# Block-causal attention with a gated MLP on one core: transposes behind the row maxima, transfers at once, an earlier first MLP, spread weight work

## The chip, the core and the metric

The kernel runs on one core of a Trainium2 chip. The time is device microseconds of one execution. The engines are named as in the profile: PE (TensorE, matrix products; PEld its weight loads), DVE (VectorE), ACT (ScalarE), POOL (GpSimd) and SP (SyncE, which here only issues transfers). Each engine executes its own instruction list in order; a semaphore makes an instruction wait for work of another engine.

## What is computed

For 8 batches and 8 heads (S = 576 positions, 64 numbers per head), scores = q kT / 8 with a mask by blocks of 64 (a row of block i sees the blocks up to i), softmax over a row, product with v. The heads side by side are x, 576 x 512 per batch. Then the gated MLP:

```python
h = np.maximum(x @ w_in, 0.0)               # 512 -> 1024
u, v = (h[..., :d_ff // 2], h[..., d_ff // 2:])
mu = np.mean(v, axis=-1, keepdims=True)
var = np.mean((v - mu) ** 2, axis=-1, keepdims=True)
v_n = (v - mu) / np.sqrt(var + 1e-06)
v_s = np.einsum('ts,bsd->btd', w_spatial, v_n) + b_spatial[None, :, None]
gated = u * v_s
return (gated @ w_out).astype(np.float32)   # 512 -> 512
```

Most products are made in three parts: an operand is split into a high part (a rounded copy, made by ACT) and a low part (the rest, made by POOL or DVE), and high x high, high x low and low x high are summed in PSUM.

## The kernel before

**Pairs and slots.** A batch has four pairs of heads; pair (b, p) is done in seven slots (`NS = 7`), one per step of the loop over `n`. Slots 0 to 5 are row tiles 0-1, 2 and 3 of the one and of the other head, slot 6 is what is left of both heads (two halves of 288 columns). For a slot PE makes the scores (L285, L297), DVE the row maximum (L320, or L329 for slot 6; `exps`), which also copies the scores out of PSUM into a tile p, ACT the exponential (L336), DVE the sum and its reciprocal (L347, L350; `norm`), POOL the scaling of p (L354), DVE the transpose in 32 x 32 blocks into a tile q (`transposes`, L406, L411). When a pair has all its slots transposed, 16 transfers (`move`, L421) put the quarters of q into place in the one buffer `turned`, from which PE makes the product with v (`av`, L464 and L481). ACT and DVE take that out of PSUM as high and low part of x (`x_evac`, L439, L443). Batch 0 and the very last pair transpose on PE instead (`transposes_pe`, L383) and have the scores from unsplit operands (batch 0). Scores have four PSUM banks, which are taken in turn; all other products share four more. Tiles p have five buffers, `turned` one.

**The MLP.** A batch has 29 groups of matmuls: five of v (`v_group`, L512, L522), eight of u (L606), eight of the spatial product (`sp_group`, L630 to L635) and eight of the output (L665). `begin(b)` puts them in a queue; in each step a credit grows by `rate` and lets groups go, so that the MLP of one batch lies between the scores of the next. What follows a group on the other engines is put into later steps with `later(steps, phase, f)`, and `due(phase)` carries it out at four places of a step. After a v group ACT evacuates (L530), DVE makes the statistics (L542, L543 and a chain of small instructions), ACT normalises (L566) and copies the high part, DVE makes the low part (L582; L586 for the fifth group, whose 64 rows go to `vs_a` and `vs_b`). The tiles of v before normalisation, tag `vr`, share their buffers with the weights that are being converted.

**Weights and operands.** `spread(gen, count, first, last)` deals the sub-steps of a generator evenly over steps. The weights are 64-bit words; DVE converts them to 32 bits (L145 to L158), ACT makes the high part and POOL the low part (L122, L124). `prep_pair` splits the next pair's operands (ACT L240, POOL L243).

**Order.** The program is written in steps, but a scheduler that knows the dependencies puts the instructions of each engine into the order in which they stand; on the chip that order is fixed. The step's core is:

```python
            exps(*here, i)
        if at(n - 1) and (i - 1) % NS in (1, 3, 5, 6):
            norm(*at(n - 1))
        due(1)
        step_background(n)
```

## Time and profile before

| | |
|---|---|
| median of 3 runs | 764.27 us (762.53 to 765.03) |
| profiled execution | 762.24 us, span 760.4 us |
| PE busy | 717.2 us, 94% |
| DVE, ACT, POOL busy | 459.7, 425.8 and 339.4 us |
| transfers | 92.05 MB, mean 121 GB/s |

"Busy" leaves out issuing, branches and semaphores. The window rows that are shown below have, after the stretch and its length, the busy time of PE, PEld, DVE, ACT and POOL with the number of instructions, the granted clock of TensorE (1.00 is full), the mean share of the transfer engines, and GB/s. A row of waits reads: waiting engine and instruction, what it waited for, total us, count, longest. A timeline row has the start, the length, the engine, line, operation and tiles; in brackets stands how long the engine stood idle before it, and for what. Line numbers are those of the kernel before.

### The profile page before, as it was taken

The numbers are of one execution on the slowest core, as the hardware profiler recorded it, in microseconds if no ns is written. First come the engines' busy times: TensorE is split into PE (matmuls) and PEld (weight loads), VectorE is DVE, ScalarE is ACT, GpSimd is POOL, SyncE is SP. The second block draws the span as 40 slices with busy tenths as digits, with TensorE's granted clock in tenths as the row PEclk, the third lists the DMA queues.
The fourth block names the chain that finished last, engine by engine and source line by source line (L and its number), as shares of the span: only waits on it lengthen the run. The fifth ranks groups of instructions, "written<-read, shape, count | busy, mean of one in ns | idle before, by whom it ended". The sixth has DMA issues, their size and how long they took to land.

```text
span 760.4 us, 16376 instructions
## 1 busy us (share of the span) xinstructions
PE 717.2 (94%) x5729; PEld 621.4 (82%) x5729; DVE 459.7 (60%) x1587; ACT 425.8 (56%) x1156; POOL 339.4 (45%) x525
## 2 busy tenths in 40 slices
PE   8879858999989999899999999899998999999998
PEld 5647747888878888798888988798887988899897
DVE  6985876556676557756665557756576557621430
ACT  6877754445654555655565556754566556642542
POOL 4788456553325633555136534355335551231011
PEclk9999969899999999999999999999999999999999
DMA  6443624355435554455353753345553552341001
GB/s 215 163 151 96 185 89 135 91 157 161 111 93 145 160 159 102 105 151 143 107 136 94 198 146 92 110 135 146 157 136 86 152 156 65 97 105 41 7 16 47
DMA packets 42150, 92.05 MB, mean 121 GB/s; under 512 B 9298, under 2 KB 18002, under 8 KB 42068
## 3 DMA queue, kind: packets, MB, share of 16 engines
q1 hardware_dynamic: 32852, 81.56, 39.1%
q10 hardware_dynamic: 9216, 9.44, 3.7%
q8 instruction: 45, 0.74, 0.4%
q14 instruction: 37, 0.30, 0.1%
HBM read 38.18 MB, written 9.44 MB: 63 GB/s over the span
## 4 chain that ended last, share of the span: by engine, by line
PE 50%; DVE 16%; ACT 15%; POOL 10%; issue 6%; DMA 1%; SPq 0%; POOLq 0%; DVEq 0%; ACTq 0%
PE mo L665 13%; PE ms L630 11%; PE s L285 7%; ACT p L336 5%; POOL lo L243 4%; PE avh L464 4%; POOL p L354 4%; PE mv L512 4%; PE mu L606 3%; ACT vr L566 3%; DVE p L320 3%; DVE st L542 3%; DVE q L406 2%; PE avl L464 2%; PE s L297 2%
## 5 line engine op out<-in xcount | busy, mean ns | idle before, releaser
L354 POOL TENSOR_SCALAR p<-p,ssum 128x128 f32<-128x128 f32 (+4 forms) x288 | 159.0, 567 | 206.4 <-DVE ssum L350 100.1
L336 ACT ACTIVATE p<-p,nmax 128x128 f32<-128x128 f32 (+4 forms) x288 | 167.0, 581 | 87.4 <-DVE nmax L320 43.5
L406 DVE STREAM_TRANSPOSE q<-p 128x384 f32<-128x384 f32 (+1 forms) x189 | 114.0, 623 | 69.4 <-POOL p L354 65.3
L320 DVE CUSTOM_DVE_ANT_0 p<-s,mask 128x128 f32<-128x128 f32 (+3 forms) x256 | 117.8, 477 | 31.9 <-PE s L285 29.0
L243 POOL TENSOR_TENSOR lo<-raw,hi 128x288 fp32r<-128x288 f32 x112 | 94.3, 865 | 90.4 <-ACT hi L240 90.4
L606 PE MATMUL mu<-x,wi_hi 128*128 128x288 f32 x512 | 115.6, 304 | 0.0
L649 POOL TENSOR_TENSOR gl<-u,gh 128x288 fp32r<-128x288 f32 x64 | 51.4, 806 | 91.4 <-ACT gh L648 91.3
L606 PEld LDWEIGHTS mu<-x,wi_hi 128*128 128x128 f32 x512 | 86.3, 190 | 5.2 <-issue 1.2
L512 PE MATMUL mv<-wi_hi,x 128*128 128x512 f32 x256 | 85.3, 395 | 0.0
L630 PE MATMUL ms<-ws_hi,vh 128*128 128x288 f32 x256 | 77.1, 301 | 6.9 <-DVE x L443 6.9
L665 PE MATMUL mo<-gh,wo_hi 128*128 128x288 f32 x256 | 79.2, 309 | 0.0
L665 PE MATMUL mo<-gl,wo_hi 128*128 128x288 f32 x256 | 77.0, 301 | 1.7 <-POOL gl L649 1.4
L648 ACT CAST gh<-u 128x288 fp32r<-128x288 f32 x64 | 27.5, 433 | 87.9 <-DVE u L639 82.5
L285 PE MATMUL s<-hi 64*128 64x128 f32 (+1 forms) x224 | 64.5, 404 | 12.6 <-DVE nmax L329 6.1
L665 PE MATMUL mo<-gh,wo_lo 128*128 128x288 f32 x256 | 75.6, 295 | 0.0
L630 PE MATMUL ms<-ws_hi,vl 128*128 128x288 f32 x256 | 75.5, 295 | 0.0
L630 PE MATMUL ms<-ws_lo,vh 128*128 128x288 f32 x256 | 75.4, 294 | 0.0
L606 PE MATMUL mu<-x,wi_lo 128*128 128x288 f32 x256 | 70.6, 298 | 0.0
L639 DVE TENSOR_TENSOR u<-ms,u 128x288 f32<-128x288 f32 x64 | 28.3, 445 | 53.7 <-PE ms L635 53.7
L285 PEld LDWEIGHTS s<-hi 64*128 64x128 f32 x224 | 31.7, 188 | 35.5 <-issue 14.3
L512 PEld LDWEIGHTS mv<-wi_hi,x 128*128 128x128 f32 x256 | 48.1, 188 | 11.3 <-ACT st L545 1.5
L464 PE MATMUL avh<-turned,v 128*64 128x128 f32 x868 | 56.7, 285 | 0.0
(120 smaller groups left out, 1608.9 us busy)
## 6 DMA issues: line engine op xcount, KB each, us to landing
turned<-q SPq DMA_DIRECT2D x216, 100.0 KB, 2.2
turned<-q SPq DMA_DIRECT2D x216, 96.0 KB, 2.2
raw<-qk SPq DMA_DIRECT2D x31, 608.0 KB, 4.3
v<-v SPq DMA_DIRECT2D x32, 320.0 KB, 3.1
outT<-o ACTq DMA_DIRECT2D x64, 144.0 KB, 2.3
rwi<-w_in SPq DMA_DIRECT2D x8, 512.0 KB, 3.7
rwo<-w_out SPq DMA_DIRECT2D x4, 512.0 KB, 4.4
rws<-w_spT SPq DMA_DIRECT2D x4, 288.0 KB, 2.8
```

What stands on the lines that cost most here:

```text
L243: nc.gpsimd.tensor_tensor(out=lo[:, cs], in0=raw[:, cs], in1=hi[:, cs].bitcast(F32), op=ALU.subtract)
L285: nc.tensor.matmul(banks[(b, pr, i + hd)][:, o:o + n], a[js, qs], k[js, :n], start=(m == 0), stop=(m == len(parts) - 1),)
L320: nc.vector.tensor_tensor_reduce(out=pt[:, o:o + n], in0=bk[:, o:o + n], in1=mask[:, 512 - n:], scale=-0.125, scalar=BIG, op0=ALU.add, op1 ...
L336: nc.scalar.activation(pt[:, o:o + n], pt[:, o:o + n], AF.Exp, bias=mx, scale=-1.0, accum_out=ssum[:, s0 + r:s0 + r + 1],)
L354: nc.gpsimd.tensor_scalar(out=pt[:, o:o + w], in0=pt[:, o:o + w], scalar1=ssum[:, r:r + 1], scalar2=1.0, op0=ALU.mult, op1=ALU.mult,)
L406: nc.vector.transpose(to[:, :, o:o + 32 * n].rearrange("p r (c j) -> p c r j", j=32), pt[:, :n * P].rearrange("p (c r j) -> p c r j", r=4, ...
L464: nc.tensor.matmul(out[js, (t0 - q0) * P:(t1 + 1 - q0) * P].rearrange("p (t a j) -> p a t j", a=4, j=32), vt[:, c, js], src[:, :, o:o + 32 ...
L512: nc.tensor.matmul(ps, xs[k][:, j, cs], w[:, k, DH:], start=(n == 0), stop=(n == 3 * NC - 1),)
L606: nc.tensor.matmul(ps[:, :HT], w[:, k, ds], xs[k][:, j, zs], start=(n == 0), stop=(n == 3 * NC - 1),)
L630: nc.tensor.matmul(ps[:, :HT], a[:, ds], w[:, k, zs], start=(n == 0), stop=False)
L649: nc.gpsimd.tensor_tensor(out=gl[:, dc, :], in0=uz, in1=gh[:, dc, :].bitcast(F32), op=ALU.subtract)
L665: nc.tensor.matmul(ps[:, :HT], w[:, k, es], a[:, k, :], start=(n == 0), stop=(n == 3 * ND - 1),)
```

## The change

Six edits. (1) The block transposes of a pair's slot are issued one step later (`n - 3`) and directly behind the row maxima and exponentials of the step, where they stood at the end of the step. (2) The 16 transfers of a pair are issued together; they were dealt out four per step. (3) `av` is issued ahead of the maxima, and in batch 0 the evacuation of x, the copy of its tail and `begin` come a step sooner each, so that the first batch's MLP starts two steps sooner. (4) The weights' sub-steps get other ranges: the v half of w_in steps 2 to 18 (before: 3 to 20), the u half 18 to 33 (21 to 34), w_sp 33 to 40 (33 to 39); w_out has its old range. (5) In `prep_pair` both high copies are one sub-step, and the low parts start after two. (6) The tag `vr` has two buffers, before three.

```diff
@@ -31,8 +31,7 @@
-LAST, AV_AT, BOOT_AV, MOVES = 5, 2 * NS + 2, NS + 2, 4
+LAST, AV_AT, BOOT_AV = 5, 2 * NS + 2, NS + 2
@@ -137,7 +136,7 @@
-        f = ff_p.tile([P, 512], F32, tag="vr", name=f"f{name}", bufs=3)[:, :n]
+        f = ff_p.tile([P, 512], F32, tag="vr", name=f"f{name}", bufs=2)[:, :n]
@@ -238,7 +237,8 @@
         for cs in (slice(0, S), slice(S, KQ)):
             nc.scalar.copy(hi[:, cs], raw[:, cs])
-            yield
+        yield
+        yield
@@ -419,7 +419,6 @@
             for a in range(4):
                 nc.sync.dma_start(turned[32 * r:32 * r + 32, a, :w], t[32 * a:32 * a + 32, r, :w])
-                yield
@@ -444,6 +443,10 @@
+        if b == 0:
+            hi()
+            lo()
+            return
         later(1, 0, hi)
         later(1, 1, lo)
@@ -486,7 +489,7 @@
-        later(1, 2, lambda: nc.gpsimd.tensor_scalar(
+        later(1 if b else 0, 2, lambda: nc.gpsimd.tensor_scalar(
             out=tails[b][:, pr], in0=xts[(b, pr)][:, :, FULL * P:].bitcast(F32), scalar1=1.0,
             scalar2=1.0, op0=ALU.mult, op1=ALU.mult,
         ))
@@ -500,7 +503,7 @@
-            vr = ff_p.tile([P, DH], F32, tag="vr", name=f"vr_{b}_{c}", bufs=3)
+            vr = ff_p.tile([P, DH], F32, tag="vr", name=f"vr_{b}_{c}", bufs=2)
@@ -725,14 +728,13 @@
     load_pair(0, 0)
     load_v(0, 0)
     U0 = NPAIR * NS
-    spread(chain([prep_w_in(c, 1) for c in range(NC)]), 7 * NC + 1, 3, U0 - 8)
-    spread(chain([prep_w_in(c, 0) for c in range(NC)]), 7 * NC + 1, U0 - 7, U0 + 6)
-    spread(chain([prep_w_sp(c) for c in range(FULL)] + [prep_w_tail()]), 3 * FULL + 5, U0 + 5, U0 + 11)
+    spread(chain([prep_w_in(c, 1) for c in range(NC)]), 7 * NC + 1, 2, 18)
+    spread(chain([prep_w_in(c, 0) for c in range(NC)]), 7 * NC + 1, 18, U0 + 5)
+    spread(chain([prep_w_sp(c) for c in range(FULL)] + [prep_w_tail()]), 3 * FULL + 5, U0 + 5, U0 + 12)
     spread(chain([prep_w_out(c) for c in range(ND)]), 7 * ND + 1, U0 + 10, U0 + 17)
     queue = []
     rate = 0.0
     credit = 0.0
-    moving = []
 
 
     TURNS = ((), (0, 1), (), (2, 3), (), (4, 5), (6,))
@@ -771,7 +773,7 @@
             if i == LAST + 1 and g + 2 < NPAIR:
                 load_pair(0, g + 2)
             if i == 2 and b > 0:
-                spread(prep_pair(b, pr), 7, n, n + 4)
+                spread(prep_pair(b, pr), 8, n, n + 4)
         if i == 3 and NPAIR < g < len(pairs):
             load_v(*pairs[g - 1])
         if i == 4 and here == last:
@@ -786,35 +788,32 @@
                 scores(*here, (4, 5))
             elif i == LAST:
                 scores_last(*here)
+        for of in range(max(0, g - 2), min(g + 1, len(pairs))):
+            if n - of * NS == (BOOT_AV if by_pe(pairs[of]) else AV_AT):
+                av(*pairs[of])
+                if of % NPAIR == NPAIR - 1:
+                    later(1 if of >= NPAIR else 0, 3, lambda b=pairs[of][0]: begin(b))
+        if here:
             exps(*here, i)
+        if at(n - 3):
+            for j in TURNS[(i - 3) % NS]:
+                b, pr, _ = at(n - 3)
+                if not by_pe((b, pr)):
+                    transposes(b, pr, j)
+                    if j == NS - 1:
+                        move(b, pr)
         if at(n - 1) and (i - 1) % NS in (1, 3, 5, 6):
             norm(*at(n - 1))
         due(1)
         step_background(n)
-        for of in range(max(0, g - 2), min(g + 1, len(pairs))):
-            if n - of * NS == (BOOT_AV if by_pe(pairs[of]) else AV_AT):
-                av(*pairs[of])
-                if of % NPAIR == NPAIR - 1:
-                    later(1, 3, lambda b=pairs[of][0]: begin(b))
-        for gen in moving[:1]:
-            for _ in range(MOVES):
-                if next(gen, gen) is gen:
-                    moving.remove(gen)
-                    break
-        turn = [(*at(n - 2)[:2], j) for j in TURNS[(i - 2) % NS]] if at(n - 2) else []
-        for b, pr, j in turn:
-            if by_pe((b, pr)):
-                transposes_pe(b, pr, j)
+        if at(n - 2) and by_pe(at(n - 2)[:2]):
+            for j in TURNS[(i - 2) % NS]:
+                transposes_pe(*at(n - 2)[:2], j)
         credit = min(credit + rate, 2.0)
         while credit >= 1.0 and queue and queue[0][0]():
             queue.pop(0)[1]()
             credit -= 1.0
         due(2)
-        for b, pr, j in turn:
-            if not by_pe((b, pr)):
-                transposes(b, pr, j)
-                if j == NS - 1:
-                    moving.append(move(b, pr))
         due(3)
 
 
```

The order on DVE where batch 2's MLP ends its v and u groups and its spatial groups begin, under pairs (3,3) and (4,0); `ms_2_0_0` is the first spatial product, `q_3_3` the transposed p of pair (3,3), `x_3_1` the x of pair (3,1), whose PSUM banks `avl`, `avh` it frees. Before:

```order
L320 ISA p_4_0_0_4179,nmax_4_0_0_4177<-s_4_0_0_4163,mask_93 128x256
L320 ISA nmax_4_0_0_4177 128x1
L406 STREAM_TRANSPOSE q_3_3_4055<-p_3_3_4_4061 128x4x4x32
L347 TENSOR_SCALAR ssum_3_3_6_4132<-ssum_3_3_6_4132 128x1
L443 TENSOR_TENSOR x_3_1_4023<-avl_3_1_3974,x_3_1_4023 128x256
L443 TENSOR_TENSOR x_3_1_4023<-avh_3_1_3975,x_3_1_4023 128x320
L350 RECIPROCAL ssum_3_3_6_4132<-ssum_3_3_6_4132 128x1
L406 STREAM_TRANSPOSE q_3_3_4055<-p_3_3_5_4103 128x4x4x32
L639 TENSOR_TENSOR u_2_3525<-ms_2_0_0_4039,u_2_3525 128x288
```

And of the change:

```order
L442 TENSOR_TENSOR x_3_1_4052<-avl_3_1_3972,x_3_1_4052 128x256
L329 ISA p_3_3_6_4151,nmax_3_3_6_4149<-s_3_3_6_0_4117,mask_93 128x288
L329 ISA nmax_3_3_6_4149 128x1
L406 STREAM_TRANSPOSE q_3_3_4090<-p_3_3_2_4004 128x3x4x32
L329 ISA p_3_3_6_4151,nmax_3_3_6_4149<-s_3_3_6_1_4118,mask_93,nmax_3_3_6_4149 128x288
L329 ISA nmax_3_3_6_4149 128x1
L406 STREAM_TRANSPOSE q_3_3_4090<-p_3_3_3_4057 128x3x4x32
L347 TENSOR_SCALAR ssum_3_3_4_4086<-ssum_3_3_4_4086 128x2
L442 TENSOR_TENSOR x_3_1_4052<-avh_3_1_3973,x_3_1_4052 128x320
```

The two instructions that make the low half of x stood between the transposes of slots 4 and 5; now they stand ahead of the transpose of slot 4, among the row maxima of slot 6 and the transposes of slots 2 and 3.

A little earlier on DVE, the row maxima of slots 2 to 4 of pair (3,3) and the low half `vs_a` of the fifth v group of batch 2. Before:

```order
L320 ISA p_3_3_2_3962,nmax_3_3_2_3960<-s_3_3_2_3921,mask_93 128x384
L320 ISA nmax_3_3_2_3960 128x1
L560 TENSOR_SCALAR st_2_4_3825<-st_2_4_3825 64x1
L320 ISA p_3_3_3_4028,nmax_3_3_3_4027<-s_3_3_3_3922,mask_93 128x384
L320 ISA nmax_3_3_3_4027 128x1
L347 TENSOR_SCALAR ssum_3_3_0_3890<-ssum_3_3_0_3890 128x4
L350 RECIPROCAL ssum_3_3_0_3890<-ssum_3_3_0_3890 128x4
L320 ISA p_3_3_4_4061,nmax_3_3_4_4059<-s_3_3_4_3952,mask_93 128x512
L320 ISA nmax_3_3_4_4059 128x1
L586 TENSOR_TENSOR vs_a_118<-vr_2_4_3824,vs_b_119 64x512
```

And of the change:

```order
L320 ISA p_3_3_1_3943,nmax_3_3_1_3942<-s_3_3_1_3896,mask_93 128x256
L320 ISA nmax_3_3_1_3942 128x1
L589 TENSOR_TENSOR vs_a_118<-vr_2_4_3812,vs_b_119 64x512
L320 ISA p_3_3_2_4004,nmax_3_3_2_4002<-s_3_3_2_3934,mask_93 128x384
L320 ISA nmax_3_3_2_4002 128x1
L320 ISA p_3_3_3_4057,nmax_3_3_3_4056<-s_3_3_3_3935,mask_93 128x384
L320 ISA nmax_3_3_3_4056 128x1
L347 TENSOR_SCALAR ssum_3_3_0_3910<-ssum_3_3_0_3910 128x4
L350 RECIPROCAL ssum_3_3_0_3910<-ssum_3_3_0_3910 128x4
L320 ISA p_3_3_4_4087,nmax_3_3_4_4085<-s_3_3_4_3964,mask_93 128x512
L320 ISA nmax_3_3_4_4085 128x1
```

`vs_a` stood behind the maximum of slot 4 and now stands ahead of that of slot 2; the statistics of the same group, which stood among the maxima of slots 0 and 1, now all stand ahead of them. On PE the MLP groups lie one group sooner among the scores; the first output group `mo_2_0_0`, which had the next scores ahead of it, stands directly behind the spatial group `ms_2_0_3`.

On DVE in the boot, under pair (1,1), the second half of the maximum of slot 6 and the conversion of w_out (`fwo`). Before:

```order
L582 TENSOR_TENSOR vl_0_3_1164<-vr_0_3_1053,vh_0_3_1163 128x512
L543 BN_AGGR st_0_4_1153<-st_0_4_1153 64x2
L145 TENSOR_SCALAR fwo_1_1185<-rwo_1_1183 128x512
L546 TENSOR_SCALAR st_0_4_1153<-st_0_4_1153 64x1
L150 TENSOR_SCALAR rwo_1_1183<-rwo_1_1183 128x512
L552 TENSOR_SCALAR st_0_4_1153<-st_0_4_1153 64x1
L154 SCALAR_TENSOR_TENSOR fwo_1_1185<-fwo_1_1185,rwo_1_1183 128x512
L556 TENSOR_SCALAR st_0_4_1153<-st_0_4_1153 64x1
L158 SCALAR_TENSOR_TENSOR fwo_1_1185<-rwo_1_1183,fwo_1_1185 128x512
L560 TENSOR_SCALAR st_0_4_1153<-st_0_4_1153 64x1
L329 ISA p_1_1_6_1259,nmax_1_1_6_1257<-s_1_1_6_1_1215,mask_93,nmax_1_1_6_1257 128x288
L329 ISA nmax_1_1_6_1257 128x1
```

And of the change:

```order
L406 STREAM_TRANSPOSE q_1_1_1201<-p_1_1_2_1097 128x3x4x32
L585 TENSOR_TENSOR vl_0_3_1149<-vr_0_3_1032,vh_0_3_1148 128x512
L549 TENSOR_SCALAR st_0_4_1138<-st_0_4_1138 64x1
L329 ISA p_1_1_6_1272,nmax_1_1_6_1270<-s_1_1_6_1_1240,mask_93,nmax_1_1_6_1270 128x288
L329 ISA nmax_1_1_6_1270 128x1
L144 TENSOR_SCALAR fwo_0_1168<-rwo_0_1166 128x512
L555 TENSOR_SCALAR st_0_4_1138<-st_0_4_1138 64x1
L153 SCALAR_TENSOR_TENSOR fwo_0_1168<-fwo_0_1168,rwo_0_1166 128x512
L559 TENSOR_SCALAR st_0_4_1138<-st_0_4_1138 64x1
L157 SCALAR_TENSOR_TENSOR fwo_0_1168<-rwo_0_1166,fwo_0_1168 128x512
```

Before, the conversion of the second piece, `fwo_1`, stood ahead of the second half of the maximum; now the first piece, `fwo_0`, stands behind that half, and `fwo_1` comes after the transposes of pair (1,1). On POOL the first low half of w_sp stands ahead of the scaling of slot 4 of pair (0,3) and two of the four low halves of pair (1,1) ahead of that of slot 6, where before all four were behind it.

## The prediction

> **What bounds the kernel now.** I read the busy shares first, then equal stretches of 20 us, then what TensorE waited for in the stretches that fall short.
>
> ```profile
> PE 717.2 (94%) x5729; PEld 621.4 (82%) x5729; DVE 459.7 (60%) x1587; ACT 425.8 (56%) x1156; POOL 339.4 (45%) x525
> ```
> ```profile
> 80.00:100.00 20.00, 13.88 (x81) 11.83 (x81) 16.01 (x48) 15.32 (x38) 11.41 (x13) 0.89 0.58 156
> 100.00:120.00 20.00, 15.03 (x105) 13.22 (x106) 17.25 (x56) 11.53 (x31) 8.93 (x13) 0.60 0.26 81
> 120.00:140.00 20.00, 17.59 (x138) 15.28 (x138) 12.33 (x49) 10.17 (x31) 13.59 (x21) 0.83 0.38 107
> ...
> 300.00:320.00 20.00, 17.73 (x160) 15.42 (x159) 14.38 (x54) 14.07 (x41) 8.00 (x14) 1.00 0.45 119
> 320.00:340.00 20.00, 20.00 (x180) 18.22 (x179) 11.52 (x42) 10.14 (x30) 11.81 (x19) 1.00 0.49 136
> ```
>
> TensorE is the bound: 717.2 of 760.4 us. In a window row the columns after the length are the busy times of PE, weight loads, DVE, ACT and POOL, then the granted clock and the DMA share. In 320:340 PE is full at clock 1.00, so a change can win nothing there. What can be won is where PE idles or runs at half clock: the stretch in which batch 0's MLP is done under batch 1's first pairs, 80 to 140, and the seam between two batches (300:320 lacks 2.27 us, and the like returns in every batch). The first of these I cut from the first MLP matmuls to the end of the AV products of pair (1,2), and then by its half-clock pieces:
>
> ```profile
> 62.40:159.00 96.60, 82.16 (x615) 70.19 (x613) 66.09 (x220) 55.86 (x150) 54.56 (x75) 0.86 0.47 131
> ```
> ```profile
> 88.60:92.10 3.50, 3.50 (x17) 3.50 (x16) 3.47 (x13) 3.44 (x9) 1.15 (x2) 0.51 0.97 255
> 98.90:116.00 17.10, 11.03 (x75) 9.22 (x75) 14.28 (x49) 8.48 (x24) 6.75 (x11) 0.50 0.19 68
> 133.00:139.80 6.80, 6.80 (x63) 6.08 (x62) 4.72 (x18) 4.20 (x11) 4.58 (x8) 0.50 0.00 1
> ```
>
> PE idles 96.60 - 82.16 = 14.4 us there, and 3.50 + 11.03 + 6.80 = 21.3 us of matmuls run at half clock, half of it, 10.7 us, lost: 25 us is the most that this stretch can give. The waits of PE between 62 and 160 and those of DVE between 78.8 and 128.3 (total, count, longest) name DVE:
>
> ```profile
> PE s L285 <- DVE nmax L329: 6.1, 2, 5.5
> PE s L297 <- DVE nmax L320: 4.5, 3, 2.0
> ```
> ```profile
> DVE q L406 <- POOL p L354: 8.0, 7, 3.9
> DVE fwo L145 <- POOL wo_lo L124: 1.9, 1, 1.9
> ```
>
> Scores wait for a free PSUM bank, which the row maxima (L320, L329) release; the maxima stand behind instructions in DVE's queue that themselves wait for POOL. Two of these stalls, in the timeline:
>
> ```profile
> 99.58 0.43 DVE L145 TENSOR_SCALAR fwo<-rwo 128x512 f32<-128x512 f32 x1 [1.95 <-POOL wo_lo L124]
> 101.95 0.50 DVE L329 CUSTOM_DVE_ANT_0 p<-s,mask,nmax 128x288 f32<-128x288 f32 x1
> ...
> 124.74 0.71 DVE L406 STREAM_TRANSPOSE q<-p 128x512 f32<-128x512 f32 x1 [3.86 <-POOL p L354]
> ```
> ```profile
> 102.51 0.69 PE L285 MATMUL s<-hi 64*128 64x384 f32 x1 [5.50 <-DVE nmax L329]
> ```
>
> The conversion of w_out waits 1.95 us, the maximum behind it ends at 102.45, and PE, which stood 5.50 us, goes on at 102.51.
>
> At the seams (the rows of waits are for 290 to 640, which has four of them):
>
> ```profile
> PE ms L630 <- DVE x L443: 6.6, 4, 1.7
> PE s L285 <- DVE nmax L320: 1.6, 8, 0.2
> PE s L297 <- DVE nmax L320: 1.5, 4, 0.4
> ```
> ```profile
> 317.06 0.71 DVE L406 STREAM_TRANSPOSE q<-p 128x512 f32<-128x512 f32 x1 [1.41 <-POOL p L354]
> 317.72 0.41 DVE L443 TENSOR_TENSOR x<-avl,x 128x256 fp32r<-128x256 f32 x1
> ```
> ```profile
> 318.19 0.40 PE L630 MATMUL ms<-ws_hi,vh 128*128 128x288 f32 x1 [1.66 <-DVE x L443]
> ```
>
> A transpose waits 1.41 us for POOL's scaling, the low half of x behind it frees the AV bank late, and the first spatial matmul stands 1.66 us. A seam costs (6.6 + 1.6 + 1.5)/4 = 2.43 us.
>
> **The change part by part.** The sum is made against the profiled execution, 762.24 us (760.4 span and 1.84 around it); the median of the runs shown, 764.27, is 2.03 above it.
>
> *Transfers at once.* SP's order has the sixteen transfers of a pair in one block before and after:
>
> ```profile
> 291.41 10.05 SPq L421 DMA_DIRECT2D turned<-q  x16
> ```
>
> They leave one behind the other in 10.05 us already, no other transfer is moved past them from batch 1 on, so 0 (their cover is a pair of scores and MLP groups; the bounds are 0 and one transfer's share, 10.05/16 = 0.6 us, either way). The end of the program keeps its order: 0.
>
> *Preparation of weights earlier, in batch 0.* POOL now has the first low half of w_sp ahead of the scaling of slots 4 of pair (0,3), and two low halves of pair (1,1) ahead of that of slot 6:
>
> ```profile
> L124 POOL TENSOR_TENSOR ws_lo<-rws,ws_hi 128x576 fp32r<-128x576 f32 x4 | 5.7, 1437 | 0.0
> ...
> L243 POOL TENSOR_TENSOR lo<-raw,hi 128x288 fp32r<-128x288 f32 x84 | 66.9, 822 | 90.4 <-ACT hi L240 90.4
> ```
>
> That is 1.44 + 2 x 0.82 = 3.08 us of POOL work put before scalings that the last AV of batch 0 needs. One low half of w_in leaves that place, and the earlier evacuation of x lets the MLP's first matmuls stand directly behind the AV. Bounds 0 and +3.1; half, since one of the two is under the scores that DVE and ACT are still working on: **+1.5**.
>
> *Transposes a step later, in batch 1's first pairs.* Removed from DVE's way: 8.0 us of transposes that wait for POOL and 1.9 of the conversion that waits for w_out's low half, 9.9 in all; by the 5.50 us row PE gets such time back. What comes back: POOL's w_out low halves now stand ahead of scalings in three places (the last pieces of pair (1,1), slots 2 and 3 of pair (1,2)), at the length of this row, and two buffers of vr instead of three make the third, fourth and fifth group of v wait for the low half of an earlier one:
>
> ```profile
> 122.74 1.29 POOL L124 TENSOR_TENSOR wo_lo<-fwo,wo_hi 128x512 fp32r<-128x512 f32 x1
> ```
> ```profile
> L582 DVE TENSOR_TENSOR vl<-vr,vh 128x512 fp32r<-128x512 f32 x32 | 23.1, 723 | 20.5 <-ACT vh L574 20.4
> ```
>
> 3 x 1.29 + 3 x 0.72 = 6.0. From batch 1 on the two buffers cost nothing, since a group of v comes only every second group (order "vuvu"), and the five buffers of p still hold the pieces that wait a step longer. Net 6.0 - 9.9 = **-3.9**, with bounds 0 (everything returns) and -9.9.
>
> *From 128 to 159.* Here PE idles 2.41 us in 120:140 and 3.4 of its 6.8 us at half clock are lost. The idle is in the same queue behind the 3.86 us transpose. Bounds 0 and -5.8; I take a third, **-2.0**, because the half clock goes away only if the idle ahead of it does, and I have just left more than half of that in place.
>
> *The seams.* The low half of x now stands ahead of the last transposes, so the 1.66 goes, if those transposes are late with no one behind them; late next is only the move of the pair to `turned`, which has the following steps. Against it stand two moves. First, every MLP group lies one group sooner among the scores, so the statistics of the fifth group of v and the low half vs_a are ahead of the row maxima of slots 2 to 4 of the fourth pair:
>
> ```profile
> 309.85 0.87 DVE L586 TENSOR_TENSOR vs_a<-vr,vs_b 64x512 fp32r<-64x512 f32 x1 [0.87 <-ACT vs_b L576]
> ```
>
> It holds DVE 0.87 and may wait another 0.87 there: 1.74 us in front of maxima for which the scores of slot 6 and of the next pair wait. Second, the first output group stands directly behind the last spatial group, as it did once in batch 0, where it waited for POOL's split:
>
> ```profile
> 145.64 0.40 PE L665 MATMUL mo<-gl,wo_hi 128*128 128x288 f32 x1 [0.34 <-POOL gl L649]
> ```
>
> The new seam costs at least this 0.34, and at most 0.34 + 1.74 and the 0.78 of waits for maxima that stand there now, 2.86. I take 1.7, above the middle, because nothing in DVE's queue lies between vs_a and the maxima that it delays, so only an MLP group on PE can cover it. A seam then gives 2.43 - 1.70 = 0.73 (bounds -2.1 and +0.4 on the time); with the first seam near 217, taken at the same, five give -3.65, and the extra 0.34 of the last batch makes **-3.3**.
>
> Sum: +1.5 - 3.9 - 2.0 - 3.3 = -7.7, so 754.5 for an execution like the profiled one and 756.6 for the median.
>
> [...] The clock falls after idle pieces far shorter than a window:
>
> ```profile
> 217.74 0.49 PE L285 MATMUL s<-hi 64*128 64x512 f32 x1 [1.41 <-DVE st L546]
> 219.69 0.40 PE L297 MATMUL s<-hi 128*128 128x288 f32 x1 [1.00 <-DVE nmax L320]
> ```
> ```profile
> 218.40:221.80 3.40, 2.40 (x17) 1.62 (x14) 2.28 (x11) 2.59 (x9) 1.62 (x4) 0.99 0.00 0
> 221.80:225.20 3.40, 3.40 (x29) 3.02 (x30) 2.50 (x6) 1.99 (x6) 1.14 (x2) 0.50 0.02 5
> 315.00:318.40 3.40, 1.74 (x13) 1.50 (x12) 1.99 (x9) 2.94 (x10) 3.40 (x6) 1.00 0.65 153
> ```
>
> 1.41 and 1.00 us of idle, two us apart, were followed by 3.4 us at 0.50, a loss of 1.7; one idle of 1.66 at the later seam by none (320:340 has 1.00). So a seam of 1.7 us in several pieces may or may not set it off; my sum has no such loss. [...]
>
> **The rivals.**
> (A) *The waits only move.* POOL is as busy as before, and DVE waits for POOL at the transposes wherever they stand; the next transposes stop the next maxima. For it: what I let come back is already 6.0 of 9.9, and the 1.74 at the seams is nearly the 1.66 that goes. Against it: in the new order the maxima of a step precede its transposes. Gains of at most 2 us: about **763**.
> (B) *The seam gets longer.* DVE stands at the fifth group's chain with the row maxima behind it. ACT needs 0.80 to normalise and twice 0.62 to copy before vs_a can go:
>
> ```profile
> 308.21 0.80 ACT L566 ACTIVATE vr<-vr,st 64x512 f32<-64x512 f32 x1
> 309.72 0.62 ACT L577 CAST vs_a<-vr 64x512 fp32r<-64x512 f32 x1
> ```
>
> 2.04 and 0.87 of DVE are 2.9 us, 0.5 more than the whole seam now, and with the 0.78 of old waits and the 0.34 of the output group a seam is 4.0, that is 1.6 more, and then each is followed by half clock for 1.7. Four seams cost 4 x 3.3 = 13.2, less the 4.4 of the boot: 762.2 + 8.8 = 771, **773** for the median. It decides as soon as idle at a seam passes about 2.4 us within some 4 us. [...]
> (C) *The boot stalls go wholly.* With the maxima ahead of every stall, the idle of the long stretch falls below what throttles it: of the 25 us about 16 come back, and the seams' 3.3: **745**. Against it: POOL's 3.1 and 6.0 us above.
>
> **How the numbers follow.** The forecast 756.6 has chance 0.47, with its own range 752 to 762 from the bounds of the boot; A 0.20, B 0.20, C 0.13. About 0.3%, 2.3 us, is what a measurement here can tell from no change, so "the same" is 762 to 766.6. Faster is the forecast and C, 0.60; the same is A, 0.18 with a little of it given to slower; slower is B and that rest, 0.22. The range takes in half of B's way and C to its middle: 746 to 771.
>
> **What would show it.** Right: the rows in which `ms` waits for x vanish and a wait of `mo` for gl of about 0.3 appears at every seam; DVE has no wait for wo_lo at the conversion of w_out ahead of a maximum; the stretch from the first MLP matmul to the AV of pair (1,2) gets 4 to 8 us shorter, with its clock above 0.86; the first `mv` starts 1 to 2 us later. Wrong: half clock at the seams (B); transposes that still wait some 8 us with maxima behind them in the boot (A); a third buffer of vr missed, seen as ACT's vr waiting for vl from batch 1 on, where I have put nothing; or the AV of a pair waiting for `turned`, which I have called covered.

## The result, and the profile after

The changed kernel takes 756.57 us in the median (754.73 to 759.79, six runs), the kernel before 763.91 beside it (761.76 to 765.03): a ratio of 0.9913, with a 95% interval of 0.9885 to 0.9940. A second series gave 757.63 us and 0.9910 (0.9885 to 0.9934). The forecast was 756.6. The number came out; the way to it did not, as the stages show at once.

I cut both profiled executions at the same points of the program: the starts of the products with v of pairs (0,3), (1,2), (3,0) and (7,0). The window rows have the columns explained with the profile before. First the kernel before, then the changed one:

```profile
0.00:62.40 62.40, 51.41 (x384) 33.97 (x384) 48.35 (x167) 47.01 (x132) 44.61 (x65) 0.95 0.49 164
62.40:156.00 93.60, 79.19 (x558) 67.34 (x557) 63.09 (x212) 54.77 (x146) 54.56 (x75) 0.85 0.46 126
156.00:288.50 132.50, 129.22 (x1038) 112.31 (x1038) 83.48 (x295) 73.07 (x202) 59.61 (x96) 0.99 0.49 137
288.50:640.10 351.60, 341.74 (x2818) 299.63 (x2818) 223.53 (x789) 200.47 (x553) 159.41 (x256) 1.00 0.48 130
640.10:760.40 120.30, 115.62 (x936) 108.17 (x935) 41.29 (x127) 50.51 (x127) 21.16 (x33) 1.00 0.19 53
```
```profile
0.00:66.40 66.40, 53.25 (x386) 36.23 (x386) 45.67 (x167) 47.59 (x134) 44.61 (x67) 0.87 0.50 159
66.40:157.00 90.60, 77.17 (x572) 66.42 (x570) 65.29 (x213) 54.74 (x144) 54.40 (x76) 0.87 0.44 127
157.00:292.30 135.30, 130.61 (x1038) 113.81 (x1038) 83.57 (x298) 74.25 (x205) 59.40 (x95) 0.97 0.49 134
292.30:638.50 346.20, 342.76 (x2819) 301.03 (x2818) 225.81 (x789) 200.28 (x553) 159.28 (x256) 1.00 0.48 131
638.50:758.00 119.50, 113.96 (x924) 106.71 (x923) 40.52 (x123) 49.20 (x123) 21.12 (x33) 1.00 0.20 53
```

Up to the AV of pair (3,0) the changed kernel is 3.8 us **later** (292.3 against 288.5), and 3.4 in the profile of the second series. Some 1.7 us of that is work brought forward: the second stage has 14 matmuls more and the last 12 fewer, one MLP group. The rest is idle and half clock. It is not lost everywhere: the stage from (0,3) to (1,2), in which the forecast had its boot gain, is 3.0 us shorter (4.9 in the second profile) even with that group more in it. The stage ahead of it is 4.0 us longer (5.2), and the one behind it, which has the first seam, 2.8 (3.1). The four batches between (3,0) and (7,0) take 346.2 for 351.6, and 344.6 in the second profile; the first has one stretch of half clock of 3.4 us in it. Without that it is some 1.7 us a batch. The end is 0.8 shorter, with the one group less in it; its idle time grew from 4.7 to 5.5 us. So the whole gain came from the later seams, while the forecast put all five at 3.3 us, and the boot, which was to give 4.4, lost. The profiles differ by 2.4 and 4.4 us from the one before, the medians by 7.3 and 6.4: the profiled execution before was 1.7 under the median of its six runs.

The larger waits of TensorE in the four batches of the changed kernel (waiting instruction, what it waited for, total, count, longest):

```profile
PE s L285 <- DVE nmax L320: 1.8, 5, 0.4
PE mo L668 <- POOL gl L652: 1.2, 4, 0.3
```

The four waits of 1.66 for x are gone. By the window rows a batch idles (346.20 - 342.76)/4 = 0.86 us where it idled (351.60 - 341.74)/4 = 2.47. Ahead of (1,2) and at the first seam there are new stalls. On PE, and on DVE ahead of the first of them:

```profile
120.61 0.47 PE L285 MATMUL s<-hi 64*128 64x128 f32 x1 [5.41 <-DVE nmax L320]
...
141.84 0.61 PE L668 MATMUL mo<-gh,wo_hi 128*128 128x288 f32 x1 [4.06 <-ACT gh L651]
...
223.05 0.47 PE L285 MATMUL s<-hi 64*128 64x128 f32 x1 [2.23 <-DVE nmax L320]
```
```profile
114.73 0.95 DVE L144 TENSOR_SCALAR fwo<-rwo 128x512 f32<-128x512 f32 x1 [0.95 <-POOL lo L243]
115.60 1.01 DVE L149 TENSOR_SCALAR rwo<-rwo 128x512 int32<-128x512 int32 x1
116.53 0.57 DVE L406 STREAM_TRANSPOSE q<-p 128x384 f32<-128x384 f32 x1
117.03 1.18 DVE L153 SCALAR_TENSOR_TENSOR fwo<-fwo,rwo 128x512 int32<-128x512 int32 x1
118.13 0.56 DVE L406 STREAM_TRANSPOSE q<-p 128x384 f32<-128x384 f32 x1
118.62 1.25 DVE L157 SCALAR_TENSOR_TENSOR fwo<-rwo,fwo 128x512 int32<-128x512 int32 x1
119.80 0.16 DVE L347 TENSOR_SCALAR ssum<-ssum 128x2 f32<-128x2 f32 x1
119.87 0.68 DVE L320 CUSTOM_DVE_ANT_0 p<-s,mask 128x512 f32<-128x512 f32 x1
```

The stall before was 5.50 us behind the second piece of w_out; now it is 5.41 behind the fourth, whose four conversions and 0.95 us wait stand ahead of the maximum of slot 5 of pair (1,2). The wait moved to another piece of the same work. The 2.23 us at the first seam are followed by 6.8 us of half clock; before, 1.41 and 1.00 us there were followed by 3.4.

### The profile page after: what moved, and what is told of

Its sections match the earlier page's. It is cut to its first block, busy times and chain, and to the rows that moved or that the text cites. A ratio compares the mean times of both kernels' runs of the same rounds, so it can differ in the third digit from the quotient of the medians.

```text
span 758.0 us, 16374 instructions
## 1 busy us (share of the span) xinstructions
PE 717.8 (95%) x5729; PEld 624.2 (82%) x5729; DVE 460.9 (61%) x1587; ACT 426.1 (56%) x1156; POOL 338.8 (45%) x525
## 4 chain that ended last, share of the span: by engine, by line
PE 48%; DVE 20%; ACT 13%; POOL 9%; DMA 4%; issue 4%; SPq 1%; POOLq 0%; DVEq 0%; ACTq 0%
PE mo L668 12%; PE ms L633 8%; PE s L285 8%; POOL p L354 4%; PE avh L467 4%; ACT p L336 4%; DVE q L406 4%; PE mu L609 3%; DVE st L545 3%; PE mv L515 3%; PE avl L467 2%; DVE p L320 2%; POOL gl L652 2%; POOL lo L243 2%; ACT vr L569 2%
## 5 line engine op out<-in xcount | busy, mean ns | idle before, releaser
L354 POOL TENSOR_SCALAR p<-p,ssum 128x128 f32<-128x128 f32 (+4 forms) x288 | 162.5, 583 | 206.4 <-DVE ssum L350 135.4
L609 PE MATMUL mu<-x,wi_hi 128*128 128x288 f32 x512 | 112.8, 299 | 0.3 <-DVE x L442 0.3
L668 PE MATMUL mo<-gh,wo_hi 128*128 128x288 f32 x256 | 81.6, 319 | 4.1 <-ACT gh L651 4.1
L668 PE MATMUL mo<-gl,wo_hi 128*128 128x288 f32 x256 | 79.4, 310 | 4.3 <-POOL gl L652 3.3
L668 PE MATMUL mo<-gh,wo_lo 128*128 128x288 f32 x256 | 77.2, 302 | 0.0
L668 PEld LDWEIGHTS mo<-gh,wo_hi 128*128 128x128 f32 x256 | 49.6, 194 | 9.9 <-ACT gh L651 4.5
L668 PEld LDWEIGHTS mo<-gl,wo_hi 128*128 128x128 f32 x256 | 49.7, 194 | 9.1 <-POOL gl L652 8.9
```

Source lines behind the costliest of these rows:

```text
L354: nc.gpsimd.tensor_scalar(out=pt[:, o:o + w], in0=pt[:, o:o + w], scalar1=ssum[:, r:r + 1], scalar2=1.0, op0=ALU.mult, op1=ALU.mult,)
L609: nc.tensor.matmul(ps[:, :HT], w[:, k, ds], xs[k][:, j, zs], start=(n == 0), stop=(n == 3 * NC - 1),)
L668: nc.tensor.matmul(ps[:, :HT], w[:, k, es], a[:, k, :], start=(n == 0), stop=(n == 3 * ND - 1),)
```

## The experiments

All times are medians, each ratio is to runs of the kernel before beside it on the same chip (whose medians lie between 763.5 and 765.0); "AV (3,0)", "four batches" and "end" are the stages above, of one profiled execution each.

| run | median us | ratio to before (95%) | AV (3,0) at | four batches | end |
|---|---|---|---|---|---|
| kernel before | 763.91 | 1 | 288.5 | 351.6 | 120.3 |
| changed kernel | 756.57 | 0.9913 (0.9885 to 0.9940) | 292.3 | 346.2 | 119.5 |
| changed kernel again | 757.63 | 0.9910 (0.9885 to 0.9934) | 291.9 | 344.6 | 119.5 |
| late MLP | 765.54 | 1.0019 (1.0003 to 1.0035) | 292.2 | 352.0 | 120.4 |
| old transposes | 774.42 | 1.0130 (1.0109 to 1.0151) | 286.8 | 360.4 | 123.8 |
| only the transposes | 758.36 | 0.9920 (0.9901 to 0.9940) | 284.7 | 351.8 | 120.3 |
| transposes and MLP | 755.04 | 0.9879 (0.9853 to 0.9906) | 289.2 | 346.4 | 119.5 |
| old weights | 757.41 | 0.9916 (0.9892 to 0.9941) | 291.6 | 344.5 | 119.5 |
| old splitting | 758.29 | 0.9928 (0.9905 to 0.9950) | 291.0 | 344.6 | 119.4 |
| three buffers of vr | 753.21 | 0.9864 (0.9836 to 0.9893) | 289.1 | 346.1 | 119.5 |
| transposes, vs_a on POOL | 746.71 | 0.9777 (0.9752 to 0.9802) | 280.7 | 344.8 | 121.0 |
| three buffers, vs_a on POOL | 753.65 | 0.9865 (0.9840 to 0.9890) | 288.2 | 344.8 | 120.1 |
| three buffers, w_out wide | 751.03 | 0.9822 (0.9796 to 0.9847) | 285.7 | 344.7 | 119.5 |
| transposes, vs_a on POOL, w_out wide | 749.49 | 0.9804 (0.9779 to 0.9829) | 279.2 | 345.0 | 121.0 |

**Where the seams' gain comes from.** Two theories stood against each other: A, that the gain is the earlier MLP's, which puts the release of x ahead of the late transposes; B, that it is the moved transposes'. First the changed kernel again, with an A and a B of its own:

> The changed kernel once more, for a second profile of it. Its first profile was of an execution of 759.79 us, 3 us above its median: a batch took 86.2 us there against 87.9 before, and the boot up to the fourth seam 3.6 us more than before. Theory A (the gain is all at the seams, 1.7 us each, and the boot gives nothing on average): a batch takes 86.2 us again, the start of pair (2,1)'s scores is within 2 us of where it was before, and the time is 755 to 758. Theory B (the boot gives 4 us in a typical execution and the first profile was an unlucky one): the same point is 3 us or more earlier than before. Both: ratio to the kernel before 0.990 to 0.993.

That A held: 86.15 us a batch, and a boot that gives nothing on balance (291.9 at (3,0)). Then the changed kernel with the first MLP at its old steps:

```diff
-        if b == 0:
-            hi()
-            lo()
-            return
...
-        later(1 if b else 0, 2, lambda: nc.gpsimd.tensor_scalar(
+        later(1, 2, lambda: nc.gpsimd.tensor_scalar(
...
-                    later(1 if of >= NPAIR else 0, 3, lambda b=pairs[of][0]: begin(b))
+                    later(1, 3, lambda b=pairs[of][0]: begin(b))
```

> The changed kernel with batch 0's MLP back at its old steps: x is taken out of PSUM, its tail copied and the queue filled one step later each. Everything else as changed, the transposes a step later behind the maxima too. In the order of the instructions the MLP groups lie where they did before, and the low half of x stands behind the transpose of slot 4 again. Theory A (the seams' gain comes from the MLP lying one group sooner, which puts the release of x's bank ahead of the late transposes): a batch takes 87.5 to 88 us again, the spatial group waits 1.2 to 1.7 us for x, and the time is 761 to 765. Theory B (it comes from the transposes being behind the maxima): a batch stays at 86.2 to 86.7 and the time at 756 to 758.5.

A batch takes 88.0 us again, as A said, and the time is 765.5, half a microsecond above A's range; but not by the wait that A named: no spatial group waits for x there. The changed kernel with the transposes back at the end of the step before:

```diff
-        if at(n - 3):
-            for j in TURNS[(i - 3) % NS]:
-                b, pr, _ = at(n - 3)
-                if not by_pe((b, pr)):
-                    transposes(b, pr, j)
-                    if j == NS - 1:
-                        move(b, pr)
+        if at(n - 3):
+            b, pr, j = at(n - 3)
+            if j == NS - 1 and not by_pe((b, pr)):
+                move(b, pr)
...
         due(2)
+        if at(n - 2):
+            for j in TURNS[(i - 2) % NS]:
+                b, pr, _ = at(n - 2)
+                if not by_pe((b, pr)):
+                    transposes(b, pr, j)
```

> The changed kernel with the transposes back at the end of the step before (the transfers stay where the change has them). In the order the low half of x stands ahead of the transpose of slot 4, as in the change, but the transposes stand ahead of the maxima of the next step. Theory A: the spatial group does not wait for x, a batch takes 86.2 to 87 us, time 756 to 759. Theory B: transposes that wait for POOL hold the maxima again, a batch takes 87.5 us or more and the time is above 761.

It is the slowest of all, 774.4 us, 90.1 a batch. Its waits of TensorE in the four batches:

```profile
PE s L285 <- DVE nmax L320: 4.8, 4, 1.2
PE s L297 <- DVE nmax L320: 4.0, 4, 1.0
PE mo L668 <- POOL gl L652: 3.1, 8, 0.8
```

B was right here: with the MLP one group sooner, transposes in the old place hold up the maxima. (On TensorE the first scores of the next pair also changed places with the AV in this order, so it is not the transposes' place alone.) The kernel before with only the transposes moved:

```diff
             exps(*here, i)
+        if at(n - 3):
+            for j in TURNS[(i - 3) % NS]:
+                b, pr, _ = at(n - 3)
+                if not by_pe((b, pr)):
+                    transposes(b, pr, j)
+                    if j == NS - 1:
+                        moving.append(move(b, pr))
...
-        for b, pr, j in turn:
-            if not by_pe((b, pr)):
-                transposes(b, pr, j)
-                if j == NS - 1:
-                    moving.append(move(b, pr))
```

> The kernel before with only the transposes moved a step later and behind the maxima; nothing else of the change. The order at the seam is the same as in the run with the late MLP. Theory A: the seam keeps its 1.2 to 1.7 us wait for x and loses at most the 0.8 us of waits for maxima: 760.5 to 764. Theory B: 756 to 758.5. In the boot, by the prediction's term, the transposes' 8 us of waits leave the maxima's way and up to 4 us are won there; by the first profile of the changed kernel nothing is.

758.4 us, which neither theory gets to in the right way: the batches gain nothing (351.8), and the whole gain is in the boot. Stages up to the AV of (1,2), and the seam, on DVE and PE:

```profile
0.00:62.30 62.30, 52.28 (x384) 34.90 (x384) 48.63 (x167) 46.78 (x132) 44.60 (x66) 0.92 0.49 164
62.30:150.90 88.60, 77.52 (x558) 65.32 (x556) 65.29 (x211) 54.55 (x146) 55.29 (x75) 0.87 0.49 133
```
```profile
304.40 0.78 DVE L586 TENSOR_TENSOR vs_a<-vr,vs_b 64x512 fp32r<-64x512 f32 x1 [1.09 <-ACT vs_b L576]
305.22 0.69 DVE L320 CUSTOM_DVE_ANT_0 p<-s,mask 128x512 f32<-128x512 f32 x1
```
```profile
305.97 0.32 PE L285 MATMUL s<-hi 64*128 64x128 f32 x1 [1.65 <-DVE nmax L320]
```

The boot is 5.1 us shorter by the AV of (1,2) (150.9 for 156.0). At the seam the wait for x has gone, and in its place the next pair's scores wait 1.65 us for the maximum of slot 4, which stands behind vs_a. So of the change's own edits the seam needs two: the moved transposes take away the wait for x, and the earlier MLP puts vs_a in front of maxima for which TensorE does not wait. (The waits of 0.36 us in the changed kernel's batches lie elsewhere: the first is at 291.61, and vs_a stands at 308.57.)

**What the boot gives back.** The late MLP with the change's other edits reaches (3,0) at 292.2, the transposes alone at 284.7: some 7 us are lost to the edits that the two do not share. Three of those, the weights' ranges, the splitting and the buffers of vr, were undone in the changed kernel, that is with the earlier MLP in place, all at once (the diffs are the change's own parts, reversed) and one by one. The transfers at once and the place of `av` ahead of the maxima stayed; no run takes them back:

> The changed kernel with three of its edits undone: the old ranges of the weights, the old splitting of a pair's operands, three buffers of vr. What is left is the moved transposes, the transfers at once and the earlier first MLP. Theory C (from the runs so far: the moved transposes win 4 to 5 us in the boot and nothing at the seams, the earlier MLP on top of them wins 1.7 us at each seam, and the three edits undone here give 7 us back in the boot): the scores of pair (2,1) start 3 to 5 us earlier than in the kernel before, a batch takes 86.2 us, and the time is 749 to 752. Theory M (the earlier MLP itself fills DVE in the boot and takes the transposes' gain there): a batch takes 86.2 us, but the boot is no shorter than in the changed kernel, 755.5 to 758.

> The changed kernel with the old ranges for w_in and w_sp alone (w_out has the same range in both). Theory W (the earlier weights are what lengthens the boot: a low half of w_sp stands ahead of the scaling that the last AV of batch 0 waits for, 1.4 us, and the w_out conversions come to lie among the maxima): 750 to 753.5. Theories P, V and M: 755.5 to 758.

> The changed kernel with the old splitting of a pair's operands alone (one high copy per sub-step, four low halves behind them, seven sub-steps). Theory P (the four low halves, issued close together and later, stand on POOL ahead of the scalings, as in the 4.1 us wait of the output group for gh near 138): 751 to 754. Theories W, V and M: 755.5 to 758.

> The changed kernel with three buffers of vr, two before. Theory V, which is the prediction's term (three waits of 0.72 us in the boot because a group of v has to wait for the low half of an earlier one): 2 us faster than the changed kernel, 754 to 755.5. Theories W, P and M: no change, 756 to 758, since in the first profile of the changed kernel the evacuation of v waited for an earlier low half only 0.06 us.

Together they are worth 2.7 us of boot there (289.2 for 291.9), not 7, in the time 0.9879 for 0.9910 to 0.9913, with intervals that overlap. The weights' ranges and the splitting each change nothing that can be told (0.9916 and 0.9928). The third buffer of vr alone gives 753.2 us, 3.4 and 4.4 less than the two series of the changed kernel; its interval and theirs overlap by a hair, and its profile agrees (289.1). So the buffer most likely costs something, and more than theory V's 2 us; but the way in which V priced it is not what the traces show, since the waits for an earlier low half are 0.06 us in the first profile and 0.13 in the second. How else the buffer acts stays open. Theory M is nearer than C, though its time of 755.5 to 758 is missed by half a microsecond and the boot is shorter than it says: with the old weights, splitting and buffers, (3,0) is at 289.2 and with the transposes alone at 284.7, of which one MLP group, 1.7 us, is work brought forward. The other 2.8 us can be the earlier MLP's, or those of the two edits that stayed. Theory C's 749 to 752 was too good.

**Taking vs_a off DVE.** If the 1.65 us is vs_a's, it must go when POOL makes it:

```diff
-                    nc.vector.tensor_tensor(
+                    nc.gpsimd.tensor_tensor(
                         out=vs_a[64:64 + m, :], in0=vr[:m, :], in1=vs_b[:m, :].bitcast(F32),
```

> The kernel before with the transposes moved and, new, the low half of the fifth v group (vs_a) made by POOL and not by DVE; otherwise as the run with the transposes alone. There every seam has a wait of 1.65 us of the next pair's scores for a row maximum, and vs_a stands on DVE just ahead of that maximum, 1.09 us of it waiting for ACT's copy. Theory vs_a: taken off DVE's queue the 1.65 goes and nothing takes its place: seam idle below 0.6 us, a batch at 85.9 to 86.4 us without half clock, 749 to 753 in all. Theory x: the same time is then lost one step on, where the spatial group waits for the low half of x that stands behind the transpose of slot 4 (1 to 1.7 us, as in the kernel before): a batch stays at 87 to 88 us, 756 to 759.

746.7 us, the fastest kernel of the study, 2.2% under the one before, with two edits and not six. Its stages to (1,2) and (3,0) and the four batches, and what TensorE waits for in the latter:

```profile
63.90:151.70 87.80, 76.89 (x558) 65.15 (x557) 64.14 (x211) 54.57 (x145) 56.34 (x76) 0.88 0.48 133
151.70:280.70 129.00, 126.43 (x1039) 110.58 (x1039) 83.50 (x294) 73.32 (x202) 61.16 (x97) 1.00 0.51 141
280.70:625.50 344.80, 340.09 (x2817) 299.02 (x2816) 225.16 (x785) 199.33 (x553) 164.83 (x260) 1.00 0.49 132
```
```profile
PE ms L630 <- ACT u L615: 3.8, 4, 1.0
PE s L285 <- DVE nmax L320: 0.8, 4, 0.2
```

```profile
308.65 0.40 PE L630 MATMUL ms<-ws_hi,vh 128*128 128x288 f32 x1 [0.94 <-ACT u L615]
```
```profile
309.00 0.39 DVE L443 TENSOR_TENSOR x<-avl,x 128x256 fp32r<-128x256 f32 x1
```

The 1.65 us waits are gone. In their place the spatial group waits 0.95 us, for ACT's evacuation of the last u group and not for x, whose low half is made only after that group has begun (309.00 against 308.65). Theory vs_a holds in its cause, not in its sizes: the time is below its 749 to 753, and a batch still idles (344.80 - 340.09)/4 = 1.18 us where it had less than 0.6. Of the 13.9 us between this profile and the one before, 4.3 are won up to (1,2), 3.5 in the stage with the first seam, where the clock is now 1.00, and 6.8 in the four batches; the end gives 0.7 back. On the changed kernel the same edit should do little, if vs_a delays nobody there:

> The changed kernel with three buffers of vr and vs_a made by POOL. With the MLP one group sooner the maxima that vs_a delays are ones that TensorE does not wait for, apart from 0.36 us at the start of the fourth pair. Both theories: 0 to 2 us faster than the same kernel with vs_a on DVE, so 751 to 754; if POOL's vs_a, at 0.8 to 1.3 us, holds up the scalings behind it, up to 2 us slower.

753.65 us against 753.21: nothing. The waits of 0.36 us in the batches are there as before, and the scores of the next pair at the first seam wait 2.38 us. So neither is vs_a's; ahead of the maximum that ends the latter DVE waits for ACT's exponential (1.92 us in this run, 0.98 in the changed kernel).

**The conversions of w_out.** Last, the preparation of w_out over ten steps instead of seven:

```diff
-    spread(chain([prep_w_out(c) for c in range(ND)]), 7 * ND + 1, U0 + 10, U0 + 17)
+    spread(chain([prep_w_out(c) for c in range(ND)]), 7 * ND + 1, U0 + 10, U0 + 20)
```

> The changed kernel with three buffers of vr and the preparation of w_out spread over steps 38 to 48 and not 38 to 45. In the run with three buffers TensorE stands 5.12 us near 111 behind a maximum that has the conversions of the third and fourth piece of w_out ahead of it on DVE, and 4.03 us near 133 for gh. Theory: with one piece in place of two ahead of that maximum the 5.12 falls by 2 to 4 us, time 749 to 752. Rival: the stall goes to the next maximum (slot 5, behind the fourth piece), or w_out's last low half comes too late for the first output group; 752.5 to 756.

751.0 us; the longest wait for a maximum, 5.12 us, falls to 1.3, and the wait for gh stays. The waits of TensorE between 65 and 160, and the stage from (0,3) to (1,2), with three buffers alone, and then with w_out wide as well:

```profile
PE s L285 <- DVE nmax L320: 6.4, 3, 5.1
PE mo L668 <- ACT gh L651: 4.0, 1, 4.0
```
```profile
65.00:152.20 87.20, 75.98 (x572) 65.62 (x571) 64.42 (x213) 54.25 (x144) 55.11 (x75) 0.88 0.47 131
```
```profile
PE s L285 <- DVE nmax L320: 4.3, 5, 1.3
PE mo L668 <- ACT gh L651: 4.1, 2, 3.8
PE s L297 <- DVE nmax L320: 2.0, 2, 1.3
```
```profile
65.90:150.30 84.40, 73.70 (x573) 63.14 (x571) 63.04 (x213) 54.01 (x144) 56.33 (x75) 0.94 0.47 135
```

That is 2.2 us less than with three buffers alone, the stage being 2.8 shorter; the two intervals just overlap. The waits for maxima are as long in sum as before (4.3 + 2.0 for 6.4), in seven pieces and not in three, so in that the rival is right. What got shorter is mostly TensorE's busy time, 73.70 for 75.98, at a granted clock of 0.94 for 0.88. On the fastest kernel:

> The best kernel so far (the kernel before, with the transposes moved and vs_a on POOL) with the preparation of w_out spread over steps 38 to 48 and not 38 to 45. There TensorE stands 5.11 us near 98 behind a row maximum that has the second piece of w_out on DVE ahead of it; now that piece stands behind two more pairs of maxima. Theory: 2 to 4 us faster, 743 to 745. Rival: the pieces that come later stop the maxima of slot 6 of the same pair instead, 746 to 748; if the last low half of w_out were late for the first output group, above 748.

The profile is 1.3 us shorter (745.2 for 746.5), the median 749.5 and the ratio 0.9804 to 0.9777, with overlapping intervals. No gain can be told, and whether there is a loss is left open.

## Why the prediction was right in its number, point by point

The forecast was -7.7 for an execution, and the medians moved by 7.3 and 6.4 (the profiles by 2.4 and 4.4). That the number is near is luck: errors of opposite sign cancel. **The seams**, -3.3: the profiles show 5.4 and 7.0 us over the four batches, against 4 x 0.73 = 2.9 in the sum. The step that failed is a term of the new seam: I took 1.7 us for it, 1.36 of them for vs_a and the maxima behind it, because nothing stands between the two. What I did not ask is when TensorE needs the banks which those maxima free: in the changed kernel it does not wait for them, in the kernels with the late MLP 1.65 us. I also put the blame on the wrong edit. It is the moved transposes that set vs_a in front of a maximum that counts, and the earlier MLP cures it. The other terms held: the wait for x went, and the output group's wait for gl is 1.2/4 = 0.3 us, 0.34 forecast.

**The boot**, +1.5 - 3.9 - 2.0. The transposes' two terms, -5.9 together, came out when made alone: 5.1 us at the AV of (1,2). In the whole change they are still there in their own stage, 3.0 and 4.9 us with one MLP group of some 1.7 us more in it. The steps that failed lie on either side. Ahead of it the +1.5, with a bound of 3.1, was too small: the AV of (0,3) comes 4.0 and 5.2 us later. In part that is the mechanism of the term, TensorE's transposes waiting for POOL's scaling, here from the start to the AV of (0,3) before and after:

```profile
PE t L383 <- POOL p L354: 4.9, 6, 1.9
```
```profile
PE t L383 <- POOL p L354: 8.7, 9, 3.3
```

In the second profile it is 6.6, and there all of the loss is busy time (57.7 us for 51.4) at a clock of 0.85 for 0.95. A delay is also there as early as the first AV (22.9 and 23.6 us for 19.5), which the term, made for the last AV of batch 0, did not look at. With the weights, the splitting and the buffers undone together the AV of (0,3) is at 62.8, with one alone undone at 66.3, 67.8 and 65.0, so more than one of them takes part; my sum has each edit acting by itself. Behind the stage the sum had nothing but one seam's gain of 0.7, and 2.8 and 3.1 us were lost: I priced the first seam like the later ones, and it got worse (2.23 us in one wait with 6.8 of half clock; 2.50 with the transposes alone, none for a maximum of slot 4 with vs_a on POOL besides). The output groups, for which I had 0.34 us in view, wait 4.06 for gh in batch 0; the run with the late MLP has that wait too (4.15) and the one with the old weights has not, so it is not the earlier MLP's alone. The two buffers of vr, 2.2 us, seem to cost 3.4 to 4.4, with intervals that just overlap.

**The signs.** The waits for x went and those for gl came, as forecast, and the clock of the stage is above 0.86 (0.87 and 0.90). The first `mv` starts 3.0 and 4.5 us later, not 1 to 2, and from there to the AV of (1,2) it takes 2.0 and 4.2 us less, where I had 4 to 8. A's sign came in part: between 60 and 160 DVE's transposes wait 7.5 us for POOL's scaling, the longest 2.2, where it was 15.6 and 3.9.

**Transfers at once**: no run tells them apart from the rest; with them the batches still gain their full 1.7. **Rivals.** A, that waits only move, is what happened in the boot (5.50 to 5.41 us, two pieces of w_out later). B's mechanism, vs_a with the maxima behind it and then half clock, is real, in the runs with the late MLP and with the transposes alone: there it eats the seams' gain, at 1.65 us, with the transposes alone half clock behind three of four, where I had reckoned 4.0 and always half clock. B's 2.4 us of idle within some 4 us was my estimate, from the 1.41 and 1.00 us at the first seam; the runs show no such limit, since single stalls of 1.62 to 1.65 us had half clock behind them. C's clean boot did not come in any run; the fastest kernel, near C's 745, has two thirds of its gain from the first seam on.

## What to carry to other kernels

An instruction that waits for another engine was paid for here by what stood behind it in its queue, and only where TensorE was on time for that: vs_a ahead of a maximum cost it 1.65 us a seam with the transposes alone, while in the changed kernel with three buffers of vr taking vs_a off DVE gave nothing (753.65 us for 753.21). Before charging a delayed release, ask when its bank is next wanted. Edits that move work into the same stretch need not add: test them singly, since here one moved operation and one changed engine gave more (2.2%) than six edits together (0.9%). And a total that agrees with the forecast says nothing on the terms until the stages are laid side by side.

## What the runs showed of the hardware that was not expected

**DVE next to POOL.** In the changed kernel the same conversion takes 0.65 us or 1.64 us:

```profile
107.51 0.65 DVE L153 SCALAR_TENSOR_TENSOR fwo<-fwo,rwo 128x512 int32<-128x512 int32 x1
```
```profile
110.30 1.64 DVE L153 SCALAR_TENSOR_TENSOR fwo<-fwo,rwo 128x512 int32<-128x512 int32 x1
```
```profile
110.11 1.28 POOL L123 TENSOR_TENSOR wo_lo<-fwo,wo_hi 128x512 fp32r<-128x512 f32 x1 [5.68 <-DVE ssum L350]
```

The short one ran while POOL stood idle, 5.68 us up to 110.11. The long one began while POOL made a low half, and ended 0.55 us after that low half did (111.94 and 111.39). Of the 16 conversions of w_out in this profile, the nine with POOL idle took 0.39 to 0.42 us (L144, L149) and 0.65 to 0.69 (L153, L157), the seven beside work on POOL 0.77 to 1.64. The conversions ahead of the 5.41 us stall, 0.95 to 1.25 us, are among the seven; the transposes between them keep their 0.57. Not every one beside POOL's work is longer: in the kernel before, two beside a low half took 0.68 and 0.69. By these rows a conversion placed beside POOL's splits costs up to 1 us more (1.64 for 0.65), which was not in my sum. No run took this apart from the order, and what decides the length is not shown.

**The clock.** In the run with only the transposes, each of the four seams has the same single stall of 1.62 to 1.65 us; three were followed by 3.4 us of half clock, one by none. In the profiles of the kernel before and of the changed one all changes of the granted clock lie on a grid of 3.41 us: the stretches at half clock are 3.41, 6.83, 10.24 and 17.07 us long. By such a grid, around the first and the third stall:

```profile
304.15:307.56 3.41, 1.76 (x18) 1.31 (x17) 2.85 (x8) 2.46 (x7) 2.53 (x5) 1.00 0.00 0
307.56:310.98 3.42, 3.42 (x42) 3.42 (x40) 3.42 (x15) 2.39 (x6) 1.37 (x2) 0.50 0.00 0
```
```profile
478.23:481.65 3.42, 2.81 (x19) 2.00 (x18) 2.26 (x10) 3.42 (x11) 1.48 (x4) 1.00 0.21 86
481.65:485.06 3.41, 2.40 (x30) 2.12 (x32) 3.11 (x12) 1.85 (x6) 1.72 (x3) 1.00 0.00 0
485.06:488.47 3.41, 3.41 (x53) 3.34 (x48) 2.91 (x14) 2.95 (x9) 2.17 (x3) 1.00 0.21 50
```

The first stall lies in one window of the grid, 52% busy, and half clock fills the next; the third is divided between two, 82% and 70% busy, and none follows. In these two the place on the grid goes with the outcome. Other rows do not follow it: in the kernel before three windows with a stall of 1.63 to 1.66 us were 51% to 52% busy and full clock followed, and in the changed kernel half clock followed a window that was 86% busy:

```profile
496.08:499.49 3.41, 2.94 (x16) 2.00 (x15) 0.14 (x2) 0.88 (x3) 1.95 (x3) 1.00 0.34 80
499.49:502.91 3.42, 3.42 (x16) 3.14 (x17) 0.90 (x6) 1.39 (x5) 1.54 (x4) 0.50 0.36 97
```

In the run with only the transposes three stalls of this size in four thus lost 1.7 us more, half of 3.41. With that its four batches gain nothing: TensorE idles 2.5 us less in them than in the kernel before (7.4 for 9.9) and is busy 2.7 us longer (344.4 for 341.7). What decides stays open.
